# Attention block on one core: queries and keys projected without padding by pairs of head groups, turned by a transposing DMA; values by group pairs

## The chip, the cores and the metric

The kernel runs on one core of one Trainium2 chip. The metric is the device time of one execution in microseconds (us); less is better. The engines are TensorE (PE; its weight loads are listed as PEld), VectorE (DVE), ScalarE (ACT), GpSimd (POOL) and SyncE (SP), which issues the DMAs of this kernel.

## The reference

A transformer block over 2048 rows of 640 elements: layer norm, attention with 32 heads of 20 elements, and a gated bilinear layer of width 1728, both with a residual. All inputs are bf16.

```python
x = A_x                                             # 1 x 2048 x 640
h = x + _A_ref(_layernorm(x), A_wqkv, A_wo)
h2 = h + _B_ref(_layernorm(h), B_w_gate, B_w_up, B_w_down)

def _A_ref(x, wqkv, wo):                            # H = 32, Dh = 20
    q, k, v = ...                                   # (x @ wqkv), split and by heads
    scores = einsum("bhqd,bhkd->bhqk", q, k) * Dh ** -0.5
    o = einsum("bhqk,bhkd->bhqd", softmax(scores), v)
    return o.reshape(B, S, D) @ wo

def _B_ref(x, w_gate, w_up, w_down):
    return ((x @ w_gate) * (x @ w_up)) @ w_down
```

## The kernel before, in words

**Layout.** The 32 heads form eight groups of four (`NG`, `HPG`). A head has a slot of 32 partitions (`SLOT`), 20 of them used, so a group fills 128 partitions. `kT[g]` holds the keys of group g turned: 128 partitions by 2048 rows. `qa[g]` holds the queries of rows 0 to 1535 in the same way, `qb[g]` those of rows 1536 to 2047. `vx[t]` holds the values of the 128 rows t, heads side by side, each with a column of ones behind its 20 elements, which gives the sums of the softmax. `lnT` holds the normed rows turned: five chunks of 128 columns of the model by 2048 rows.

**Projections.** For queries and keys the weights are first padded from 20 to 32 columns a head (`wpad`, filled by `pad_half` on ACT and POOL), so that one projection comes out in slots. `job_proj(m, g, ch)` makes the queries (m = 0) or keys (m = 1) of group g for block ch of 512 rows: five matmuls with `wpad` as weights and 512 columns of `lnT`, and one DVE eviction at L310 from PSUM to `kT` or `qa`/`qb`. The eviction adds a constant: keys get one in partition 20 of each slot (`one_row`), queries 544 (`shift_row`), so that each score comes out raised by 544. `job_V(t, half)` makes the values of 128 rows for sixteen heads: five matmuls with `lnT` as weights and 320 columns, cast into `vx[t]` at L268 by `evac`. All these jobs, and the transposes on PE, use the single PSUM bank of pool `mip`; the first keys of group 1 use `accp`.

**Rows.** The layer norm of a block of 512 rows runs in pieces on DVE, with a few small steps on POOL (`gen_ln`, L206 to L259). The normed rows of the blocks 0 and 1 are turned on PE (`job_T`, L281), those of the blocks 2 and 3 by transposing DMAs from SP (`turn`, L910).

**Scores.** A tile holds 1536 columns of scores, three units of 512 columns or six of 256. `emit_S` issues its score matmuls (L550) into one of two PSUM tiles `sc`; ACT takes the exponential of a whole tile (L566) into an `E` buffer; `emit_AV` multiplies with `vx` into `acc` (L787). For some tiles DVE takes the last 512 columns in place of ACT, by four operations of its own (`emit_x`: L602, L612, L613, L607). Whether it does is decided by `x_takes`: among other things DVE must not be behind PE by the program's own clock, at most two such pieces may be open, and for groups that are divided over blocks none is started while row statistics are left (`aux`) or in the last `X_CHUNK` tiles of the group.

**Order.** The order of all instructions is fixed when the program is built. The row block of queries 0 comes first ("pass 0"): for its groups 0 to 3 the keys are taken in four blocks of 512 rows, all four groups in block 0, then in block 1, and so on, with partial results in `parts` (memory of `qa`); then groups 4 to 7 over all keys; then the other passes. The loop over tiles places jobs from the queue `jobs` between the score matmuls as long as its clock (`at`) says that PE would be idle; `ensure` runs jobs at once where a tile needs their result. For each kind of work the clock has a cost, such as 216 ns a matmul of 512 columns. Sums of the softmax go through DRAM to rows and back (`norm`: L658, L659, L671, L674 on SP, L669 and L677 on DVE). The loads of `wo` (L983) are issued in the last part of pass 0, and `spill` copies the queries to DRAM for a fallback.

## Time and profile before

| | |
|---|---|
| Time, median of 3 runs | 898.12 us (897.2 to 899.1) |
| Profiled execution | 895.98 us, span 894.2 us |
| PE busy | 800.1 us (89%) |
| DVE busy | 760.1 us (85%) |
| ACT busy | 853.5 us (95%) |
| POOL busy | 33.6 us (4%) |
| Moved by DMA | 60.48 MB |

The span runs from the first to the last instruction of the profiled execution; the time has some 1.8 us around it. A share is that of the span in which an engine ran at least one instruction. Lines such as L310 are those of the kernel before.

### The profile page before, as it was taken

The page shows a single profiled execution, that of the slowest core. Times are in us where ns is not written, and L with a number is a line of the kernel's source. Part 1 is how long each engine was busy: PE and PEld are TensorE (multiplying, and loading weights), DVE is VectorE, ACT ScalarE, POOL GpSimd, SP SyncE. Part 2 cuts the span into 40 slices and gives each one's busy share as a digit, 9 for nine tenths or more (in the row PEclk, how much of TensorE's full clock was granted, in tenths as well). Part 3 has the DMA queues.
Part 4 walks back from the last instruction along what each step waited for, and adds up shares of the span by engine and source line. Part 5 has one row for each costly group of instructions (what it writes and reads, how often), then busy time and mean ns, then how long its engine had stood idle before and what let it go on. Part 6 is the DMA issues. An engine that isn't in the chain of part 4 may idle for free.

```text
span 894.2 us, 21880 instructions
## 1 busy us (share of the span) xinstructions
PE 800.1 (89%) x8861; PEld 373.1 (42%) x8919; DVE 760.1 (85%) x1415; ACT 853.5 (95%) x719; POOL 33.6 (4%) x126
## 2 busy tenths in 40 slices
PE   7888999988988899989899988988889999889997
PEld 5333233222223344544344544433434455435466
DVE  7778899999999999799999998999899888994443
ACT  6999999999999999999999999999999999999951
POOL 4100000000001100001000000001000000100000
PEclk9999999999999999999999999999999999999999
DMA  6030010011024655432224334111542203011310
GB/s 199 23 65 3 1 29 25 15 37 28 14 67 120 132 147 190 121 89 67 58 60 109 81 96 109 45 31 30 132 111 74 73 14 79 12 34 39 89 38 18
DMA packets 112107, 60.48 MB, mean 68 GB/s; under 512 B 39320, under 2 KB 108996, under 8 KB 112000
## 3 DMA queue, kind: packets, MB, share of 16 engines
q1 hardware_dynamic: 112000, 59.01, 25.3%
q8 instruction: 72, 1.18, 0.5%
q14 instruction: 35, 0.29, 0.1%
HBM read 48.09 MB, written 7.28 MB: 62 GB/s over the span
## 4 chain that ended last, share of the span: by engine, by line
ACT 61%; PE 15%; issue 15%; DVE 9%; DMA 1%; ACTq 0%; DVEq 0%
ACT E L566 49%; ACT El L566 11%; PE sc L550 3%; PE mi L1162 2%; PE acc L787 2%; PE f L1144 2%; PE mi L303 1%; DVE xv L602 1%; DVE xt L612 1%; PE f L1211 1%; DVE xt L613 1%; PE mi L1044 1%; DVE xe L607 1%; PE mi L318 1%; DVE u L1167 1%
## 5 line engine op out<-in xcount | busy, mean ns | idle before, releaser
L566 ACT ACTIVATE E<-sc 128x1536 bf16<-128x1536 f32 (+1 forms) x560 | 696.1, 1397 | 2.5 <-PE sc L550 1.7
L550 PE MATMUL sc<-qa,kT 32*128 32x256 bf16 (+1 forms) x2176 | 203.0, 318 | 27.9 <-ACT E L566 14.8
L550 PEld LDWEIGHTS <-kT 32*128 32x128 bf16 x3136 | 86.1, 91 | 225.9 <-issue 194.3
L602 DVE TENSOR_SCALAR xv<-sc 128x512 f32<-128x512 f32 x194 | 133.9, 690 | 46.1 <-PE sc L550 43.0
L566 ACT ACTIVATE El<-sc 128x1536 bf16<-128x1536 f32 (+1 forms) x123 | 159.8, 1378 | 0.3 <-PE sc L550 0.3
L787 PE MATMUL acc<-E,vx 128*32 128x256 bf16 (+1 forms) x2255 | 156.9, 314 | 1.2 <-DVE vx L268 0.6
L607 DVE SCALAR_TENSOR_TENSOR xe<-xt,xv 128x512 int16<-128x512 f32 x194 | 131.2, 682 | 0.9
L613 DVE SCALAR_TENSOR_TENSOR xt<-xt,xv 128x512 f32<-128x512 f32 x194 | 130.2, 681 | 0.8
L612 DVE SCALAR_TENSOR_TENSOR xt<-xv 128x512 f32<-128x512 uint16 x194 | 129.1, 680 | 0.4 <-DVE ri L669 0.2
L303 PE MATMUL mi<-lnT,wp 128*128 128x512 bf16 x280 | 82.7, 381 | 8.1 <-DVE qa L310 3.4
L787 PEld LDWEIGHTS <-vx 128*32 128x32 bf16 x3136 | 61.9, 96 | 61.1 <-issue 59.5
L550 PE MATMUL sc<-qb,kT 32*128 32x256 bf16 (+1 forms) x960 | 68.4, 280 | 6.9 <-ACT E L566 4.2
L1211 PE MATMUL mi<-wd,hh 128*128 128x320 bf16 x378 | 65.5, 301 | 1.2 <-DVE xr L1215 1.1
L1162 PE MATMUL mi<-ln2T,wg 128*128 128x256 bf16 x390 | 56.7, 274 | 8.6 <-DVE u L1167 7.6
L1162 PE MATMUL mi<-ln2T,wu 128*128 128x256 bf16 x390 | 55.7, 274 | 7.2 <-DVE hh L1170 7.0
L787 PE MATMUL acc<-El,vx 128*32 128x256 bf16 (+1 forms) x579 | 59.5, 292 | 0.3 <-ACT El L566 0.3
L787 PE MATMUL acc<-xe,vx 128*32 128x256 bf16 (+1 forms) x302 | 55.4, 306 | 0.3 <-issue 0.3
L1211 PEld LDWEIGHTS <-hh 128*128 128x128 bf16 x448 | 37.9, 97 | 29.4 <-issue 18.1
L1162 PEld LDWEIGHTS <-wg 128*128 128x128 bf16 x390 | 33.7, 97 | 30.0 <-issue 25.9
L303 PEld LDWEIGHTS <-wp 128*128 128x128 bf16 x310 | 24.8, 97 | 50.6 <-issue 38.5
L1162 PEld LDWEIGHTS <-wu 128*128 128x128 bf16 x390 | 33.7, 97 | 28.3 <-issue 25.2
L1170 DVE TENSOR_TENSOR hh<-mi,u 128x512 bf16<-128x512 f32 x49 | 33.7, 688 | 13.3 <-PE mi L1162 12.7
(141 smaller groups left out, 618.4 us busy)
## 6 DMA issues: line engine op xcount, KB each, us to landing
wu<-in_B_w_up_dram SPq DMA_DIRECT2D x38, 320.0 KB
wg<-in_B_w_gate_dram SPq DMA_DIRECT2D x37, 320.0 KB
bc<-scr SPq DMA_DIRECT2D x60, 64.0 KB
bc<-scr SPq DMA_DIRECT2D x108, 32.0 KB
qsp<-qa SPq DMA_DIRECT2D x8, 384.0 KB
xr<-in_A_x_dram SPq DMA_DIRECT2D x16, 160.0 KB
out_dram<-xr SPq DMA_DIRECT2D x14, 160.0 KB
wd<-in_B_w_down_dram SPq DMA_DIRECT2D x13, 160.0 KB
```

The source lines that it names most:

```text
L303: nc.tensor.matmul(ps[:], lhsT=wslice(m, g, c), rhs=lnT[:, c, ch * QB:(ch + 1) * QB], start=(c == 0), stop=(c == KT - 1))
L550: nc.tensor.matmul(sc[:, o:o + w], lhsT=kT[g][SLOT * j:SLOT * (j + 1), kt * P:(kt + 1) * P], rhs=q_of(g, b, c0, w)[SLOT * j:SLOT * (j + 1) ...
L566: exps = nc.scalar.activation(e[:, 0:n_act], sc[:, 0:n_act], ACT.Exp, bias=EXP_BIAS, scale=SM_SCALE)
L602: took = nc.vector.tensor_scalar(v[:], ps, X_SCALE, X_BASE, ALU.mult, ALU.max)
L607: nc.vector.scalar_tensor_tensor(e[:], t[:], X_R, v[:], ALU.mult, ALU.add)
L612: lambda: nc.vector.scalar_tensor_tensor(t[:], u, X_P, u, ALU.add, ALU.mult),
L613: lambda: nc.vector.scalar_tensor_tensor(t[:], t[:], X_Q, u, ALU.add, ALU.mult),
L787: nc.tensor.matmul(acc["t"][SLOT * j:SLOT * (j + 1), 0:w], lhsT=vx[kt][:, VS * h:VS * h + SLOT], rhs=e, start=(acc["n"][j] == 0), stop=(ac ...
L1144: nc.tensor.matmul(ps[:, 0:n], lhsT=st["w", fp][k][:, c, f_cols(fp, f2)], rhs=st["ln2T"][:, c, c0:c0 + n], start=(c == 0), stop=(c == KT - 1))
L1162: nc.tensor.matmul(ps[:, f2 * n:(f2 + 1) * n], lhsT=st["w", fp][k][:, c, f_cols(fp, f2)], rhs=st["ln2T"][:, c, c0:c0 + n], start=(c == 0), ...
L1170: nc.vector.tensor_tensor(st["hh"][fp][:, :, c0 % HW:c0 % HW + n], two(ps[:, 0:2 * n]), two(u[:, 0:2 * n]), ALU.mult)
L1211: nc.tensor.matmul(ps[:, 0:HALF], lhsT=st["hh"][f // 2][:, f % 2, t * P % HW:t * P % HW + P], rhs=late["Wd"][f][:, cs], start=(f == 0), st ...
```

## The change

Queries and keys of the first block of 512 rows and of the groups 0 and 1 are projected as before (`DIRECT = 2`), with padded weights for these two groups alone. All others are made by `job_pair` for two groups and 256 rows at once: `lnT` is the weights, the unpadded query or key weights of eight heads (160 columns) are streamed, ten matmuls in all. DVE casts the 320 columns into one of five padded tiles `stages`, in which the constant already stands in element 20 of each slot, and SP turns the tile by a transposing DMA of 128 x 512 into `kT`, `qa` or `qb`. These now hold two groups each, in an order of row tile, group, row. The constant is 23.25 on both sides, so that the scores are raised by 23.25 squared. Values are made by `job_vp` for two groups and 256 rows, ten matmuls of 160 columns, with one cast. The queries of the later row blocks are made for the groups 4 to 7 first. The program's clock takes a turned tile as readable 2.4 us after its eviction (`MOVE_NS`). The unpadded weights get memory of their own in place of that of `E` and `wo`; POOL sets the constants of the five tiles and some more of the values' borders.

```diff
+DIRECT = 2
+STAGES = 5
+PAIR = 2 * HPG * DH
...
+MOVE_NS = 2400
...
-SHIFT = 544.0
+ROOT_SHIFT = 23.25
...
-    qa = [qkp.tile([P, QA], BF16, name=f"qa{g}", tag=f"qa{g}") for g in range(NG)]
-    qb = [qkp.tile([P, QB], BF16, name=f"qb{g}") for g in range(NG)]
-    kT = [qkp.tile([P, S], BF16, name=f"kT{g}") for g in range(NG)]
-    vx = [vp.tile([P, VW], BF16, name=f"vx{t}") for t in range(NT)]
+    qa = [qkp.tile([P, NT - TPB, 2, P], BF16, name=f"qa{k}") for k in range(NG // 2)]
+    qb = [qkp.tile([P, TPB, 2, P], BF16, name=f"qb{k}") for k in range(NG // 2)]
+    kT = [qkp.tile([P, NT, 2, P], BF16, name=f"kT{k}") for k in range(NG // 2)]
+    vx_all = vp.tile([P, NT, VW], BF16, name="vx")
+    vx = [vx_all[:, t, :] for t in range(NT)]
...
-    wqk = [ep.tile([P, EW], BF16, name="E") for c in range(KT)]
-    wpad = [ra.tile([P, 2, H, SLOT], BF16, name=f"wp{c}") for c in range(KT)]
+    wqk = [[ra.tile([P, 2, HALF], BF16, name=f"wqk{hf}{c}") for c in range(KT)] for hf in range(2)]
+    wpad = [ra.tile([P, 2, DIRECT * HPG, SLOT], BF16, name=f"wp{c}") for c in range(KT)]
+    stages = [ra.tile([P, 4 * HPG, SLOT], BF16, name=f"st{k}") for k in range(STAGES)]
...
-        nc.gpsimd.memset(vx[t][:, hh_ * VS:hh_ * VS + SLOT - VS], 1.0)
+        for h0 in range(2 * HPG, H, 2 * HPG):
+            nc.gpsimd.memset(vx[t][:, h0 * VS:h0 * VS + SLOT - VS], 1.0)
...
+    for st in stages:
+        nc.gpsimd.memset(st[:, :, DH:VS], ROOT_SHIFT)
+        nc.gpsimd.memset(st[:, :, VS:SLOT], 0.0)
...
-    def job_proj(m, g, ch):
+    def job_proj(m, g):
...
-                nc.vector.tensor_scalar(kT[g][:, ch * QB:(ch + 1) * QB] if m else q_of(g, ch, 0, QB), ps[:],
-                                        (one_row if m else shift_row)[:, 0:1], None, ALU.add)
+                nc.vector.tensor_scalar(kT[g // 2][:, 0:TPB, g % 2, :] if m else q_of(g, 0, 0, QB), by_tile(ps[:]), shift_row[:, 0:1], None, ALU.add)
...
+    def job_pair(key, m, gp, tt, dst):
...
+        st = stages[staged["n"] % STAGES]
+        staged["n"] += 1
+        lo = gp % 2 * PAIR
+        for k in range(2):
+            for c in range(KT):
+                nc.tensor.matmul(ps[:, k * PAIR:(k + 1) * PAIR], lhsT=lnT[:, c, (2 * tt + k) * P:(2 * tt + k + 1) * P],
+                                 rhs=wqk[gp // 2][c][:, m, lo:lo + PAIR], start=(c == 0), stop=(c == KT - 1))
+                if k and c == KT - 1:
+                    evac("dve", st[:, :, 0:DH], ps[:, 0:2 * PAIR].rearrange("p (h e) -> p h e", e=DH), 408, 68)
+                    nc.sync.dma_start(dst.rearrange("p t g k -> p (t g) k"), st[:].rearrange("p h e -> p (h e)"), transpose=True)
+                    read_at[key] = at["dend"] + MOVE_NS
+                yield 68
...
+    def job_vp(gp, tt):
...
+                nc.tensor.matmul(ps[:, k * PAIR:(k + 1) * PAIR], lhsT=lnT[:, c, (2 * tt + k) * P:(2 * tt + k + 1) * P],
+                                 rhs=wv[c][:, h0 * DH:h0 * DH + PAIR], start=(c == 0), stop=(c == KT - 1))
...
-    for c in range(KT):
-        pad_half(c, 1)
...
+            add(("k0", 1), job_proj(1, 1))
+            values(0)
+            for k in range(2):
+                add_q(0, 1, k)
+            add_k(1, 0)
+            one_T()
+            add_k(1, 1)
+            one_T()
+            values(1)
             one_T()
             one_T()
+        else:
+            values(0)
+            for k in range(2):
+                add_k(1, 2 * ch + k)
+            values(1)
...
+    for gp in range(G1 // 2, NG // 2):
+        for k in range(2):
+            add_q(0, gp, k)
+        for tt in range(NT // 2):
+            add_k(gp, tt)
+            add(("vp", gp, tt), job_vp(gp, tt))
...
-    for b in range(1, NB):
-        for g in range(NG):
-            add(("q", b, g), job_proj(0, g, b))
+    for hf in (1, 0):
+        for b in range(1, NB):
+            for k in range(4):
+                add_q(b, 2 * hf + k // 2, k % 2)
```

154 lines of the change are left out of this document (73 added, 81 removed).

## Prediction

> **What bounds the kernel now.** I read the page's busy times, then the span cut into stages, then who waited for whom, and last the groups of instructions and the timelines of single engines.
>
> ```profile
> PE 800.1 (89%) x8861; PEld 373.1 (42%) x8919; DVE 760.1 (85%) x1415; ACT 853.5 (95%) x719; POOL 33.6 (4%) x126
> ACT 61%; PE 15%; issue 15%; DVE 9%; DMA 1%; ACTq 0%; DVEq 0%
> 15.00:60.00 45.00, 38.64 (x293) 14.23 (x297) 34.85 (x85) 43.17 (x33) 8.47 (x22) 1.00 0.18 45
> 60.00:131.00 71.00, 63.98 (x490) 22.74 (x493) 59.05 (x103) 71.00 (x59) 0.00 (x0) 1.00 0.08 19
> 131.00:256.00 125.00, 113.39 (x824) 34.94 (x838) 117.61 (x197) 124.57 (x104) 0.00 (x0) 1.00 0.09 21
> ```
>
> The first line is engines over the whole span, the second the shares of the chain that ended last. Each stage row is: stretch, its length, then busy us of PE, PEld, DVE, ACT, POOL, the granted clock, DMA share, GB/s. ACT, which only takes exponentials there, is busy for 71.00 of 71 us and 124.57 of 125. The three stages are those in which queries, keys and values are projected; only in the first does ACT idle, 1.83 us of 45. So a projection that gets cheaper on PE moves nothing by itself. What moves the end is how many score columns DVE takes off ACT by its own exponential (L602, L612, L613, L607), and any wait that ACT gets or loses.
>
> ```profile
> L566 ACT ACTIVATE E<-sc 128x1536 bf16<-128x1536 f32 x402 | 569.1, 1516 | 2.5 <-PE sc L550 1.7 <-PE acc L787 0.4
> L566 ACT ACTIVATE E<-sc 128x1024 bf16<-128x1024 f32 x158 | 167.7, 1092 | 0.0
> 15.00:60.00 45.00, 0.00 (x0) 1.00 0.18 45
> 60.00:131.00 71.00, 9.77 (x15) 1.00 0.08 19
> 131.00:256.00 125.00, 21.28 (x31) 1.00 0.09 21
> ```
>
> The first two rows are ACT's groups with shapes kept apart (busy us, mean ns): a tile whose last 512 columns DVE took costs ACT 1516 - 1092 = 424 ns less. The other three are the same stages for L602 alone: DVE starts none of its exponentials before 60 us, 15 in the next 71 us, 31 in the last 125. In the last stage DVE is busy for 117.61 of 125 us, so there it is DVE time that limits them. Between 15 and 131 us the rule of `x_takes` limits them (none while row statistics are in `aux`, and for the divided groups not in the last three tiles of a group): DVE idles there for 22 of 116 us.
>
> **Part by part: DVE.** 64 projections of four heads by 512 columns are made now; four of them stay as they are (groups 0 and 1, first block), 60 become 60 pair jobs of eight heads by 256 rows.
>
> ```profile
> L310 DVE TENSOR_SCALAR kT<-mi,one_row 128x512 bf16<-128x512 f32 x30 | 22.4, 746 | 5.1 <-PE mi L303 4.6
> L310 DVE TENSOR_SCALAR qa<-mi,shift_row 128x512 bf16<-128x512 f32 x23 | 17.1, 744 | 2.5 <-PE mi L303 2.3
> L268 DVE CAST vx<-mi 128x320 bf16<-128x320 f32 x32 | 15.6, 488 | 3.5 <-PE mi L318 3.3
> 71.51 0.68 DVE L612 SCALAR_TENSOR_TENSOR xt<-xv 128x512 f32<-128x512 uint16 x1
> 72.11 0.48 DVE L268 CAST vx<-mi 128x320 bf16<-128x320 f32 x1
> 72.51 0.68 DVE L607 SCALAR_TENSOR_TENSOR xe<-xt,xv 128x512 int16<-128x512 f32 x1
> 73.11 0.68 DVE L613 SCALAR_TENSOR_TENSOR xt<-xt,xv 128x512 f32<-128x512 f32 x1
> ...
> 74.12 0.69 DVE L602 TENSOR_SCALAR xv<-sc 128x512 f32<-128x512 f32 x1 [0.33 <-PE sc L550]
> 74.73 0.74 DVE L310 TENSOR_SCALAR kT<-mi,one_row 128x512 bf16<-128x512 f32 x1
> 75.39 0.68 DVE L607 SCALAR_TENSOR_TENSOR xe<-xt,xv 128x512 int16<-128x512 f32 x1
> ```
>
> Records overlap their neighbours by some 0.08 us, so I take the distance from start to start where DVE had no wait: 0.66 us for the 512-column eviction (74.73 to 75.39), 0.40 us for a cast of 320 columns (72.11 to 72.51), 0.60 us for a step of the exponential. The new eviction is a cast of 320 columns into a padded tile, for which L268 is the nearest row. DVE gains 60 x (0.66 - 0.40) = 15.6 us. One exponential is four steps, 4 x 0.605 = 2.42 us; 15.6 / 2.42 = 6.4. The values stay 32 evictions of 320 columns. Jobs that end sooner in the first 131 us pull later ones into DVE's idle time there, so most of the gain turns up behind 131 us, where DVE is the limit. I take 6 of the 6.4, since DVE is busy for 94% of that stage: 6 x 0.424 = 2.5 us off ACT. The bounds are 0 (the planner finds no tile for them) and 10 (also 10 us of the idle 22 us become usable, because the statistics end sooner): 4.2 us.
>
> **PE.**
>
> ```profile
> 7.58 0.45 PE L281 MATMUL mi<-ident,xs 128*128 128x128 bf16 x5 [1.29 <-DVE xs L259]
> 16.80 1.25 PE L303 MATMUL acc<-lnT,wp 128*128 128x512 bf16 x5
> 18.31 0.85 PE L318 MATMUL mi<-wv,lnT 128*128 128x320 bf16 x5
> L318 PEld LDWEIGHTS <-lnT 128*128 128x128 bf16 x160 | 14.1, 97 | 19.6 <-issue 16.2
> L281 PE MATMUL mi<-ident,xs x30: 217/219/230, 7.6 to 41.4; 128*128 128x128 bf16 x30
> ```
>
> A run of five takes four spacings and one duration. For 128 columns that is (0.45 - 0.219) / 4 = 58 ns with a new weight load for each. The five of 512 columns take 1.25 us, a spacing near 217 ns, the five of 320 near 137 ns. Between 58 and 137 ns, 160 columns come to 71 ns by a straight line. Ten of them are 0.71 us against 1.08 us: 60 x 0.37 = 22 us less PE time. The 32 value jobs go from five matmuls to ten, 0.68 to 0.71 us, 1 us more. On the end this is worth nothing directly, since ACT is never short of scores after 60 us; it is what lets the jobs end sooner.
>
> [...]
>
> **The transposes.** Each pair job now ends in a transposing DMA of 128x512 on SP, 60 in all. The rows' own transposes are the nearest thing, 128x640 each.
>
> ```profile
> L910 SPq DMA_TRANSPOSE lnT<-xs x8: 1199/1217/1322, 43.0 to 65.2; - x8
> 66.40:66.60 0.20, 1.00 0.94 179
> ...
> 67.00:67.20 0.20, 1.00 0.94 176
> 192.66 6.92 SPq L983 DMA_DIRECT2D wo<-in_A_wo_dram x16
> 131.00:256.00 125.00, 28.32 (x38) 1.00 0.09 21
> ```
>
> The first row is the issue time on SP (minimum, median, maximum ns, first and last start); the next two are the first and the last of four slices in which the DMA engines were busy with the last of them (share, GB/s): issued at 65.2, moved from 66.4 to 67.2. So 1.22 us of issue and 0.8 us of transfer; four fifths of both is 0.97 + 0.64 = 1.6 us from eviction to landing. The program assumes 2.4 us; I keep 1.6 to 2.4. SP gets 60 x 0.97 = 58 us of issue over 241 us. What stands ahead in SP's queue delays a transpose: the longest such block is the 16 loads of `wo`, 6.92 us. Behind it DVE could stand, because the five padded tiles are reused in turn. The last row is L310 in the last stage: 38 evictions in 125 us, one in 3.3 us; at twice that pace five tiles still last 8 us. I cost it at 0, bounded by 2 us if the pace is three times as high. The sums' trips through DRAM share that queue too, but are planned 6 us ahead; 0, within the same bound.
>
> **The start.**
>
> ```profile
> 3.75 0.33 POOL L194 MEMSET vx<- 128x11 bf16 x1
> 3.80 0.29 POOL L195 MEMSET vx<- 128x12 bf16 x1
> 7.19 2.42 POOL L200 COPY wp<-E 128x640 bf16<-128x640 bf16 x3 [3.10 <-DMA E<-in_A_wqkv_dram]
> 30.38 0.38 PE L550 MATMUL sc<-qa,kT 32*128 32x512 bf16 x1 [0.62 <-DVE kT L310]
> 30.86 14.88 ACT L566 ACTIVATE E<-sc 128x1536 bf16<-128x1536 f32 x11 [1.05 <-PE sc L550]
> 43.58 0.74 DVE L310 TENSOR_SCALAR kT<-mi,one_row 128x512 bf16<-128x512 f32 x1
> 45.15 0.39 PE L550 MATMUL sc<-qa,kT 32*128 32x512 bf16 x3
> ```
>
> POOL gets 42 more memsets in front of the weight pads. At 0.05 us each that is 2.1 us, and it stood idle for 3.10 us there; the pads halve. Cost 0; without that cover, 2.1 us. ACT loses 1.05 us at 30.86, because the scores of group 2 waited for keys that had just been made. The work ahead of those keys shrinks from 7.0 to about 6 us on PE, the evictions from 0.66 to 0.40, the landing adds 1.6 to 2.4. I take half of the idle away, 0.5 us (bounds: all of it, or 1 us more).
>
> **The sum.** 2.5 + 0.5 = 3.0 us. The profiled execution took 895.98 us (span 894.2 us and 1.78 around it), so 893.0; the median of the runs shown, 898.12, lies 2.1 above it, so 895.1. About 0.2%, 1.8 us, is what a measurement here tells from no change.
>
> **Rivals.** *Keys come late (slower).* In the first four blocks of 512 rows a pair's keys are needed soon after they are made: once in block 0 (groups 2 and 3), twice in each of blocks 1 to 3, seven places. At 30.38 the lead was nil, at 45.15, where the next block's keys are first read, 45.15 - 44.32 = 0.8 us. Where the lead stays under 1.6 us, PE stands at the scores, and ACT behind it; one such wait of 0.62 us cost ACT 1.05. At 1.0 us a place, 7 us, less the 2.5 us of DVE: +4.5, 902.6. It decides from the point at which pair jobs end less than 1.6 us ahead of their scores. Against it: per block, four value jobs and four key projections, 7.0 us of PE time, become eight jobs of 0.7 us, and each needs less of the one PSUM bank, so the lead should grow by over 1 us. [...]
>
> *DVE's time cannot be used (no change).* The tiles that DVE may take are limited by its two open tiles and by PE being ahead, not by its time; then 0 to 3 exponentials more, -0 to -1.3 us, 897.5. For it: DVE waits at L602 for scores. Against it: 94% busy.
>
> *PE gets no lighter (no change).* If each weight load of 97 ns sets the pace, 920 narrow matmuls cost 26 ns more each than 71, 24 us, all that was saved; jobs end no sooner, half the exponentials come, -1.3 us, 896.8. The burst at 58 ns speaks against it.
>
> *More than the sum.* Ten exponentials and no early idle, -4.2 - 1.0: 892.9.
>
> **The numbers.** The forecast 895.1 has 0.48, the larger gain 0.09; the two that end within 0.2% have 0.12 and 0.04; late keys 0.20, of which a fifth (0.04) would cancel the gain only; and queueing on SP 0.07, where the 2 us fall due at two or three places, 895.1 + 5 = 900.1. So faster 0.57, same 0.20, slower 0.23. The range takes in the larger gain with its bounds and most of the late keys: 892.0 to 902.6. The forecast's own range is 893.5 to 896.5.
>
> **What would show it.** Right: some 200 exponentials at L602 instead of 194, most of the new ones between 131 and 256 us; the 60 evictions near 490 ns each; 60 more transposes issued in about 1 us each; ACT idle under 1.8 us between 15 and 60 us; PE busy about 20 us less. Wrong: ACT waiting for `sc` behind a DMA into `kT` or `qa` in the first 100 us; DVE waiting for a DMA that reads the padded tiles; PE's runs of ten well over 0.9 us; the count at L602 unchanged.

## The result, and the profile after

The changed kernel takes 924.46 us in the median (922.8 to 927.28), against 898.47 us for the kernel before beside it: a ratio of 1.029 with an interval of 1.027 to 1.032. The prediction had 895.1 us. The change costs 26 us where I forecast a gain of 3. Executions of one program differ along with their mean granted clock: the kernel before took 895.45 us at 1.0 and 904.51 at 0.988, and the four of the changed kernel had 0.968 to 0.972.

The profiled execution took 922.8 us, with a span of 921.0. From here on lines are those of the kernel after: scores L594 (before L550), exponentials L611 (L566), products with the values L832 (L787), DVE's own exponential L647, L657, L658, L652 (L602, L612, L613, L607), pair jobs L344, values L365, DVE's casts L274, transposing DMAs L348. From its page, the busy times, the row of granted clocks and ACT's main group:

```profile
PE 825.6 (90%) x9474; PEld 410.0 (45%) x9474; DVE 749.9 (81%) x1427; ACT 855.4 (93%) x719; POOL 32.4 (4%) x163
PEclk9989999979999999998999999899999999999899
L611 ACT ACTIVATE E<-sc 128x1536 bf16<-128x1536 f32 (+1 forms) x559 | 694.5, 1380 | 24.9 <-PE sc L594 24.4
```

ACT does the same work (855.4 us, before 853.5), but now it stands 24.4 us in front of scores that are not there; before, that group's wait was 1.7 us. The clock row has 7 and 8 where before every digit was 9. And PE, whose work was to shrink by 20 us, is listed as busy 25.5 us longer. A part of that is only the record: the page before has 58 fewer matmuls than weight loads (8861 and 8919), the page after has all of them, and a run below with the work of before and all its records (only the order changed) lists 812.0 us. The three stages, with the columns of before:

```profile
15.00:60.00 45.00, 36.29 (x373) 18.04 (x372) 34.29 (x89) 43.18 (x32) 5.86 (x18) 0.94 0.40 76
60.00:131.00 71.00, 64.98 (x715) 35.12 (x714) 59.97 (x109) 70.39 (x59) 0.00 (x0) 0.99 0.24 46
131.00:256.00 125.00, 107.48 (x1013) 48.28 (x1011) 104.47 (x191) 113.61 (x94) 0.00 (x0) 0.95 0.30 58
```

The last two of them for L647, the first step of DVE's exponential, alone:

```profile
60.00:131.00 71.00, 10.97 (x16) 0.99 0.24 46
131.00:256.00 125.00, 21.11 (x31) 0.95 0.30 58
```

The start is as before: ACT idles 45 - 43.18 = 1.82 us, then 0.61 us. Between 131 and 256 us it idles 11.39 us, where before it idled 0.43, and the granted clock averages 0.95. DVE is freed as intended (104.47 us busy, before 117.61), yet it starts 31 of its exponentials there, as many as before.

The table load behind ACT's last exponential starts at 879.0 us; before it started at 854.24. Of these 24.8 us, 23.2 are longer waits for scores (25.2 us with those in front of `El`, before 2.0). What follows takes 42.0 us instead of 40.0. So the question is why scores come late.

One place shows how a stand comes about. The timeline of SP's queue from 173 us (start, us, instruction):

```profile
173.28 2.50 SPq L348 DMA_TRANSPOSE qa<-st  x2
175.88 1.61 SPq L716 DMA_DIRECT2D scr<-ri  x1
178.81 1.70 SPq L719 DMA_DIRECT2D bc<-scr  x4
180.61 1.41 SPq L1024 DMA_DIRECT2D wo<-in_A_wo_dram  x4
182.12 1.20 SPq L348 DMA_TRANSPOSE qa<-st  x1
183.42 1.56 SPq L1024 DMA_DIRECT2D wo<-in_A_wo_dram  x4
185.11 1.19 SPq L348 DMA_TRANSPOSE qa<-st  x1
```

DVE's timeline (with the wait in front in brackets):

```profile
184.63 0.49 DVE L274 CAST st<-mi 128x320 bf16<-128x320 f32 x1 [3.06 <-DMA qa<-st]
187.63 0.49 DVE L274 CAST st<-mi 128x320 bf16<-128x320 f32 x1 [1.19 <-DMA qa<-st]
```

PE's timeline:

```profile
182.06 0.39 PE L594 MATMUL sc<-qa,kT 32*128 32x512 bf16 x3
185.17 1.49 PE L344 MATMUL mi<-wqk,lnT 128*128 128x160 bf16 x10 [2.72 <-DVE st L274]
186.59 0.61 PE L594 MATMUL sc<-qa,kT 32*128 32x512 bf16 x3
```

ACT's timeline:

```profile
187.25 1.02 ACT L611 ACTIVATE E<-sc 128x1024 bf16<-128x1024 f32 x1 [3.04 <-PE sc L594]
189.91 1.02 ACT L611 ACTIVATE E<-sc 128x1024 bf16<-128x1024 f32 x1 [1.64 <-PE sc L594]
```

And slices of 1 us, whose third figure from the end is the granted clock:

```profile
183.00:184.00 1.00, 0.00 (x0) 0.00 (x0) 0.00 (x0) 1.00 (x1) 0.00 (x0) 1.00 0.65 129
184.00:185.00 1.00, 0.00 (x0) 0.00 (x0) 0.37 (x1) 0.21 (x1) 0.00 (x0) 0.51 0.23 46
...
193.00:194.00 1.00, 1.00 (x9) 0.72 (x7) 1.00 (x2) 0.55 (x1) 0.00 (x0) 0.50 0.50 97
...
195.00:196.00 1.00, 0.82 (x13) 0.69 (x12) 0.98 (x3) 0.97 (x1) 0.00 (x0) 1.00 0.54 104
```

DVE wants to cast into a padded tile whose transpose has not been read out yet: the tile was filled at 172.04 us, but that transpose stood in SP's queue behind a trip of the sums (175.88 to 180.51 us) and loads of `wo` until 182.12, and DVE's wait ends 2.4 us after its issue. DVE stands 3.06 us; the next pair job of PE needs the one bank that this cast frees and stands 2.72 us; the scores behind it in PE's order are late, and ACT stands 3.04 us. While PE stands, its clock falls to 0.50 and stays there for ten slices. At half clock three score matmuls take 0.61 us instead of 0.39 and the pair job 1.49 instead of some 0.86, so ACT waits again: 1.64 us behind a second, shorter stand (DVE's 1.19 us for the next tile's transpose), then 0.50 and 0.57 us with no wait for a DMA in between.

Slices at half clock lie in eight stretches before the end of the exponentials, from 54, 140, 184, 379, 413, 464, 594 and 867 us; in the profiled execution before there were none. Each lasts 3.4, 6.8 or 10.2 us in the trace's clock records. Of ACT's 25.2 us of waits, 15.0 us are waits that touch such a stretch (4.7 of them the two behind the stands just shown), 1.7 lie just ahead of one, 8.5 elsewhere. The trace shows one of two things ahead of each stretch: a stand such as the one above (140 behind DVE's wait of 1.93 us for a broadcast of the sums, with PE standing 1.90 and then 1.00 us, 184, and 379 behind PE's wait of 1.87 us for a load of `wg`), or a shortage of full-array work (54, and the ends of the passes at 413, 464, 594, 867, where PE has mostly scores, products with the values and the tiny matmuls of the sums). In the 4 us ahead of these five, matmuls of 128 rows and 128 columns are busy for 0.1 to 1.6 us; from 50 to 850 us the mean is 1.9 us in 4. What amount it takes is not shown: from 289 to 293 us they are busy for 0.6 us, and the clock stays at 1.00, as it does behind a stand of 1.61 us at 313 us.

Both kernels take their 683 exponentials in the same order, so the start of the n-th (counted from 0) can be compared. The changed kernel is level with the one before until the 80th (120 us). From the 80th to the 100th it loses 4.3 us (the stretch at 140), from the 120th to the 150th 8.0 (184), from the 280th to the 320th 5.2 (379), over the last 42 exponentials 4.4, and over all the rest 3.0. So the loss is made at a few places, not by every tile.

### The profile page after: what moved, and what is told of

Its sections match the earlier page's. It is cut to its first block, busy times and chain, and to the rows that moved or that the text cites. A ratio compares the mean times of both kernels' runs of the same rounds, so it can differ in the third digit from the quotient of the medians.

```text
span 921.0 us, 23257 instructions
## 1 busy us (share of the span) xinstructions
PE 825.6 (90%) x9474; PEld 410.0 (45%) x9474; DVE 749.9 (81%) x1427; ACT 855.4 (93%) x719; POOL 32.4 (4%) x163
## 4 chain that ended last, share of the span: by engine, by line
ACT 54%; PE 21%; issue 13%; DVE 6%; DMA 4%; SPq 1%; ACTq 0%; DVEq 0%
ACT E L611 43%; ACT El L611 11%; PE sc L594 5%; PE acc L832 3%; PE mi L344 3%; PE f L1186 2%; PE mi L544 2%; PE mi L1204 1%; DVE st L274 1%; PE f L1253 1%; PE mi L1086 1%; DMA wg<-in_B_w_gate_dram 1%; DMA xs<-in_A_x_dram 1%; DVE xt L658 1%; PE mi L365 1%
## 5 line engine op out<-in xcount | busy, mean ns | idle before, releaser
L611 ACT ACTIVATE E<-sc 128x1536 bf16<-128x1536 f32 (+1 forms) x559 | 694.5, 1380 | 24.9 <-PE sc L594 24.4
L594 PE MATMUL sc<-qa,kT 32*128 32x256 bf16 (+1 forms) x2176 | 207.6, 325 | 21.2 <-ACT E L611 15.9
L594 PEld LDWEIGHTS <-kT 32*128 32x128 bf16 x3136 | 85.4, 92 | 212.1 <-issue 166.2
L647 DVE TENSOR_SCALAR xv<-sc 128x512 f32<-128x512 f32 x197 | 135.6, 688 | 46.3 <-PE sc L594 43.1
L611 ACT ACTIVATE El<-sc 128x1536 bf16<-128x1536 f32 (+1 forms) x124 | 163.9, 1404 | 0.8 <-PE sc L594 0.8
L832 PE MATMUL acc<-E,vx 128*32 128x256 bf16 (+1 forms) x2243 | 160.0, 320 | 0.2 <-ACT E L611 0.2
L652 DVE SCALAR_TENSOR_TENSOR xe<-xt,xv 128x512 int16<-128x512 f32 x197 | 132.7, 681 | 0.8
L658 DVE SCALAR_TENSOR_TENSOR xt<-xt,xv 128x512 f32<-128x512 f32 x197 | 131.6, 680 | 0.5
L657 DVE SCALAR_TENSOR_TENSOR xt<-xv 128x512 f32<-128x512 uint16 x197 | 131.1, 682 | 0.4
L832 PEld LDWEIGHTS <-vx 128*32 128x32 bf16 x3136 | 62.5, 96 | 59.6 <-issue 56.8
L594 PE MATMUL sc<-qb,kT 32*128 32x256 bf16 (+1 forms) x960 | 69.2, 283 | 5.5 <-ACT E L611 3.7
L344 PE MATMUL mi<-wqk,lnT 128*128 128x160 bf16 x600 | 58.2, 239 | 13.1 <-DVE st L274 8.0
L1204 PE MATMUL mi<-ln2T,wg 128*128 128x256 bf16 x410 | 60.6, 277 | 10.1 <-DVE u L1209 6.4
L544 PE MATMUL mi<-kT,ident 128*128 128x512 bf16 x212 | 65.0, 388 | 4.1 <-DVE hh L1212 1.4
L1204 PE MATMUL mi<-ln2T,wu 128*128 128x256 bf16 x410 | 58.2, 273 | 10.1 <-DVE hh L1212 8.8
L1253 PE MATMUL mi<-wd,hh 128*128 128x320 bf16 x364 | 62.6, 302 | 1.5 <-DVE xr L1257 1.5
L832 PE MATMUL acc<-xe,vx 128*32 128x256 bf16 (+1 forms) x304 | 60.9, 314 | 0.0
L344 PEld LDWEIGHTS <-lnT 128*128 128x128 bf16 x600 | 43.8, 100 | 36.9 <-issue 36.5
L832 PE MATMUL acc<-El,vx 128*32 128x256 bf16 (+1 forms) x589 | 60.0, 295 | 0.0
```

What stands on the lines that cost most here:

```text
L344: nc.tensor.matmul(ps[:, k * PAIR:(k + 1) * PAIR], lhsT=lnT[:, c, (2 * tt + k) * P:(2 * tt + k + 1) * P], rhs=wqk[gp // 2][c][:, m, lo:lo ...
L544: nc.tensor.matmul(ps[:], lhsT=ident[:], rhs=kT[0][:, 0:2].rearrange("p t g k -> p (t g k)"), start=True, stop=True)
L594: nc.tensor.matmul(by_tile(sc[:, o:o + w]), lhsT=kT[g // 2][SLOT * j:SLOT * (j + 1), kt, g % 2, :], rhs=q_of(g, b, c0, w)[SLOT * j:SLOT * ...
L611: exps = nc.scalar.activation(e[:, 0:n_act], sc[:, 0:n_act], ACT.Exp, bias=EXP_BIAS, scale=SM_SCALE)
L647: took = nc.vector.tensor_scalar(v[:], ps, X_SCALE, X_BASE, ALU.mult, ALU.max)
L652: nc.vector.scalar_tensor_tensor(e[:], t[:], X_R, v[:], ALU.mult, ALU.add)
```

## The experiments

Three theories compete. **C (clock):** the change takes work from PE, PE runs out of projections early, and its clock halves. **Q (queue):** 60 transposes in SP's queue hold the five padded tiles; DVE and then PE stand. **P (plan):** the program orders all instructions by its own clock, any changed cost moves all that follows, and a part of the loss belongs to the order and not to the operations. In the tables "waits" are ACT's waits for scores in us, between 15 and 256 us and from there to 880; "tail" is the time from the last exponential to the end.

**The `wo` loads off SP.** Edit of the changed kernel:

```diff
-                nc.sync.dma_start(wo[g][SLOT * j:SLOT * j + DH, :], A_wo[DH * h:DH * h + DH, :])
+                nc.gpsimd.dma_start(wo[g][SLOT * j:SLOT * j + DH, :], A_wo[DH * h:DH * h + DH, :])
```

> The changed kernel with the 32 loads of wo issued from GpSimd in place of SyncE, which takes some 12 us of issue out of the queue of the transposes. Theory Q (the one SyncE queue holds up the padded tiles and the sums, DVE waits, PE waits behind DVE): DVE's waits for a transpose near 181 to 188 us (3.1 + 1.2 us) go, and with them the half-clock stretch of 184 to 194 us; 5 to 8 us less than 924.5, so 917 to 919. Theory C (the lighter projections leave PE too little work, and its granted clock halves wherever it runs short): the other seven half-clock stretches stay, so still over 914. If the queue were all of it, 900.

Measured: 918.24 us, ratio 1.023 (1.019 to 1.027), about 6 us better than the changed kernel, with the same order of instructions on PE. DVE no longer waits for a DMA that reads a padded tile at all, and the stretch at 184 us is gone. Between 131 and 200 us ACT's waits fall from 10.3 to 3.6 us. But the stretches at 54 and 140 us stay. So Q is worth about 6 us here, and it isn't most of the loss.

**A stricter rule for idle matmuls.** The program already issues idle matmuls: two at a time at L544 where it finds no job for PE, and one at L590 ahead of a tile's scores where by its own clock PE has had less than `FULL_NS` of full-array work, or less than `ALL_NS` of any, in the last 2.08 us. By their weight loads there were 126 + 18 of them before (the trace lacks 33 matmul records of the 126) and 212 + 27 after. The edit makes the rule of L590 stricter:

```diff
-WARM, LEAD, COOL_FROM = 58, 3, 30
+WARM, LEAD, COOL_FROM = 58, 3, 12
-FULL_IN, FULL_NS, ALL_NS = 2083, 300, 760
+FULL_IN, FULL_NS, ALL_NS = 2083, 500, 1000
```

> The changed kernel with the program's rule for warming matmuls made stricter: they start at tile 12 in place of 30, and are placed when full-array work in the last 2.08 us is under 500 ns (was 300) or, with part-array work, under 1000 ns (was 760). Theory C: the half-clock stretches at 54, 412, 463, 593 and 866 us go, those behind DVE's or a DMA's wait (139, 184, 378) stay; ACT's wait for scores falls from 24 to about 14 us; time 908 to 914. Theory Q: the stretches are a consequence of DVE's waits, so nothing changes by more than 3 us, or it gets slower by the added matmuls.

> Both edits of the two runs above together. Theories C and Q both at work, independent: the gains add, 902 to 908. C alone: as the stricter warming by itself. Q alone: as the moved loads by themselves.

Measured: alone 927.68 us, ratio 1.033 (1.028 to 1.038); together with the moved `wo` loads 916.35, 1.020 (1.016 to 1.024). Alone it is no help. It gave PE no more work either: 56 idle matmuls at L590 instead of 27, but 176 at L544 instead of 212, 232 in all instead of 239. So these two runs say little about C. With `wo` moved, the granted clock of the profiled execution rises to 0.989 (0.978 with `wo` moved alone), but the gain over moving `wo` alone is within the scatter. Waits on DMAs remain: PE 4.1 us for `ln2T`, DVE 4.4 for the sums.

**Less work on PE, and no DMA.** Edit of the kernel before, three of five matmuls in each projection except those of groups 0 and 1 in the first block, so each of the others lacks two fifths of its contraction:

```diff
-        for c in range(KT):
+        n_c = KT if g < 2 and ch == 0 else 3
+        for c in range(n_c):
```

> The kernel before with three of the five matmuls in each projection of queries and keys, the four of groups 0 and 1 in the first block excepted: 648 ns of PE in place of 1080 for 60 jobs, 26 us less PE work, with no new DMA and the old evictions. It leaves out two fifths of the contraction. Theory C: PE runs short here too, the clock halves in several stretches, and the kernel gets slower than before by 5 to 20 us. Theory Q: no transposes, no queue, so the time is that of before within 3 us, or a little less.

Measured: 906.69 us, ratio 1.009 (1.006 to 1.012): with 120 projection matmuls fewer (the program put in 83 idle ones more), and no transposing DMA added, it is 8 us slower. Its clock around 54 us, in slices of 1 us:

```profile
53.00:54.00 1.00, 0.60 (x11) 0.19 (x9) 0.90 (x3) 1.00 (x2) 0.29 (x2) 1.00 0.85 161
54.00:55.00 1.00, 0.39 (x3) 0.10 (x3) 0.34 (x1) 1.00 (x2) 0.76 (x5) 0.66 0.55 104
55.00:56.00 1.00, 0.61 (x3) 0.20 (x3) 0.07 (x1) 1.00 (x2) 0.90 (x1) 0.50 0.33 63
...
60.00:61.00 1.00, 1.00 (x8) 0.22 (x11) 0.00 (x0) 1.00 (x1) 0.00 (x0) 0.50 0.50 96
```

PE's timeline ahead of it:

```profile
49.50 0.82 PE L304 MATMUL mi<-lnT,wp 128*128 128x512 bf16 x2
50.25 0.39 PE L551 MATMUL sc<-qa,kT 32*128 32x512 bf16 x3
51.32 0.39 PE L551 MATMUL sc<-qa,kT 32*128 32x512 bf16 x3 [0.67 <-ACT E L567]
52.66 0.39 PE L551 MATMUL sc<-qa,kT 32*128 32x512 bf16 x3 [0.95 <-ACT E L567]
```

From 50.3 us PE has nothing but scores and products of 32 rows or columns of the array, waits for ACT, and 4 us later its clock halves, in the same slice and with the same 0.66 and 0.50 as in the changed kernel. No instruction on PE had waited for a late DMA there. ACT waits 4.5 us at `E` and 2.0 at `El`, more than a half of it in waits that touch the half-clock stretches. None of the seven profiled executions with full projections (the kernel before, and the runs below with the order, the values, the transposes, the short evictions and the two nudges) has a stretch near 54 us. So less work on PE is enough to halve the clock there, with no transpose about. Its price is another matter: at the 60th exponential, behind this stretch, this kernel is 0.6 us ahead of the kernel before, as the changed one is 0.2 ahead there. It loses its 8 us later, more than a half of it in the last 42 exponentials and the tail.

No gap of PE in the 4 us ahead was longer than 0.95 us, here and in the changed kernel alike (there PE was busy for 2.25 of those 4 us), so the clock halves without a long stand too.

**The order alone, and the values alone.** Edits of the kernel before:

```diff
-    for b in range(1, NB):
-        for g in range(NG):
-            add(("q", b, g), job_proj(0, g, b))
+    for hf in (1, 0):
+        for b in range(1, NB):
+            for g in range(G1 * hf, G1 * (hf + 1)):
+                add(("q", b, g), job_proj(0, g, b))
```

```diff
-            add(("v", t, 1), job_V(t, 1))
+            add(("vp", g // 2, tt), job_vp(g // 2, tt))
...
```

> The kernel before with one thing of the change alone: the queries of the later row blocks are made for the groups 4 to 7 first. Same work on every engine, same DMAs, only another order from about 190 us on. Theory C (too little PE work lets the granted clock fall): no change, 897 to 900, no half-clock stretch before the last microseconds. Theory P (the order of before happens to keep the clock up, any other order falls below the gate somewhere): two to four half-clock stretches behind 190 us and 4 to 10 us more, as with the lighter projections.

> The kernel before with the values made by group pairs (ten matmuls of 160 columns for 256 rows) and in the order that this gives; queries and keys as before. PE time and evictions are the same. Theory C and theory Q: the same time within 3 us. Theory P: 4 to 10 us more, with half-clock stretches. A PE that runs ten narrow matmuls slower than five wide ones would show as runs of over 0.9 us.

Measured: the order 899.13 us, 1.001 (0.999 to 1.003), nothing, although its profiled execution has two half-clock stretches (397 and 649 us) with PE's work as before, so such stretches come without lighter projections too; the values by group pairs 904.53, 1.007 (1.004 to 1.009). The second has no transposes, waits of only 4.0 us in all and one half-clock stretch at 573 us. Its DVE makes 190 exponentials instead of 194 (4 x 0.424 = 1.7 us), its tail is 42.3 us instead of 40.0, and DVE waits 4.6 us for sums. What of this is the value jobs' own cost and what their order's, this run cannot tell.

**Three padded tiles.**

```diff
-STAGES = 5
+STAGES = 3
```

> The changed kernel with three padded tiles in place of five. Theory Q (DVE stands at its eviction until SyncE has turned an earlier tile, PE behind DVE): DVE's waits for a transpose at its eviction grow from 5.8 us to 15 to 30 us, ACT's wait between 20 and 220 us from 14 to over 20 us, and the time is 6 to 15 us over 924.5. Theory C alone: within 3 us of it.

Measured: 931.04 us, 1.037 (1.033 to 1.041). DVE's largest wait for a DMA, in the list of waits (us in total, times, longest), here and then in the changed kernel:

```profile
DVE st L274 <- DMA qa<-st: 12.5, 8, 2.8
```

```profile
DVE st L274 <- DMA qa<-st: 5.8, 3, 3.1
```

With two tiles fewer this wait grows by 6.7 us and the time by 6.6. The program's order changes in part with it, so the near equality proves little, but the wait itself is Q's, and five tiles were already too few in that queue. More than five were not tried.

**The sums' trips off SP as well.** Edit: beside `wo`, the four steps through DRAM of each `norm` are issued by GpSimd.

```diff
-        nc.sync.dma_start(sums[:], asb[DH:P:SLOT, 0:w])
+        nc.gpsimd.dma_start(sums[:], asb[DH:P:SLOT, 0:w])
...
```

> The changed kernel with the loads of wo and also the sums' four trips through DRAM issued from GpSimd; SyncE is left with transposes, rows and weights. Theory Q: DVE's wait at 135 us for the sums, and the half-clock stretch of 139 to 146 us behind it, go as well; ACT's wait from 131 to 200 us falls from 3.6 us (with wo alone moved) to under 1; 4 to 7 us less than the 918.2 of that run, 911 to 914. Theory C: the stretches at 54 us and behind 350 us stay, so not under 908. If the GpSimd queue takes much longer for the trips, DVE waits there and the time rises instead.

Measured: 927.54 us, 1.030 (1.024 to 1.036), worse than `wo` alone by 0.7%. DVE now waits 11.0 us for the sums and 9.4 for their broadcasts. The trips got slower by GpSimd, so this says nothing about SP's queue.

**Work given back to PE.** Edits on top of the moved `wo` loads: two idle matmuls of 512 columns ahead of every pair job; then with the stricter rule (500 and 1000); then the idle ones only for keys, and later row blocks' queries, of groups 4 to 7, whose results are not needed soon.

```diff
+        for _ in range(2):
+            nc.tensor.matmul(ps[:], lhsT=ident[:], rhs=kT[0][:, 0:2].rearrange("p t g k -> p (t g k)"), start=True, stop=True)
+            yield 216
```

```diff
-        for _ in range(2):
+        for _ in range(2 if gp > 1 and (m or key[1]) else 0):
```

> The changed kernel with wo loaded from GpSimd and two idle matmuls of 512 columns put in front of each pair job, so that a pair job costs PE about 1.1 us, as a projection did before. Theory C: PE has its work back, the half-clock stretch at 54 us goes and so do those behind DVE's short waits; ACT's wait for scores up to 256 us falls from 7.4 us (wo moved alone) to 2 to 4; 904 to 912 in place of 918.2. Theory Q: only the queue matters and PE's load does not, so 916 to 920, or more, since jobs end later.

> The kernel with filled pair jobs and wo from GpSimd, and the stricter rule for warming matmuls (500 and 1000 ns in place of 300 and 760; the first tile for it stays 30). Theory C: the half-clock stretches at the ends of the later passes (about 412, 463, 593, 866 us) go as well, those behind a DMA's wait stay; 900 to 907. Theory P (the late stretches come from an order that no longer fits and not from too little work): no better than without the rule.

> The changed kernel with wo from GpSimd, the stricter rule for warming matmuls (500 and 1000 ns), and the two idle matmuls only in front of pair jobs whose result is not needed soon: keys of the groups 4 to 7, and their queries of the later row blocks. The early keys and the queries of pass 1 keep their lead. If too little PE work between 60 and 256 us and SyncE's queue are the causes there, and filling failed before only because it made early keys late: ACT's wait for scores is 3 to 5 us up to 256 us, 3 to 5 us behind it, 902 to 907 in all. If filling costs by itself, it stays over 914.

| kernel | us | ratio | waits 15 to 256 | waits 256 to 880 | tail |
|---|---|---|---|---|---|
| before | 898.47 | | 1.7 | 0.3 | 40.0 |
| after | 924.46 | 1.029 (1.027 to 1.032) | 13.8 | 11.3 | 42.0 |
| `wo` moved | 918.24 | 1.023 (1.019 to 1.027) | 7.4 | 10.3 | 42.4 |
| + filled everywhere | 927.73 | 1.034 (1.031 to 1.037) | 22.1 | 6.5 | 42.3 |
| + stricter rule | 923.19 | 1.028 (1.025 to 1.031) | 20.9 | 5.1 | 42.8 |
| filled late only, stricter rule | 905.79 | 1.007 (1.005 to 1.009) | 6.9 | 2.2 | 44.0 |

In this order, filling every pair job makes the time worse, for a reason of its own. The largest of PE's waits for a DMA in the kernel that is filled everywhere:

```profile
PE sc L597 <- DMA kT<-st: 8.9, 3, 3.8
```

and one of them in its timeline:

```profile
38.83 0.38 PE L597 MATMUL sc<-qa,kT 32*128 32x512 bf16 x1
41.96 0.61 PE L597 MATMUL sc<-qa,kT 32*128 32x512 bf16 x2 [2.74 <-DMA kT<-st]
```

The early keys come late, and ACT loses 13.6 us before 60 us. In the same kernel ACT's waits between 131 and 200 us, the stage of the stand above, fall to 0.7 us (10.3 after, 3.6 with `wo` moved), and the granted clock of that stage is 1.00 (0.90 and 0.95). With the fill left out where keys are needed at once, both come together, and the list of ACT's waits has

```profile
ACT E L614 <- PE sc L597: 9.1, 13, 1.8
```

instead of 24.4 us. This kernel still has all 60 transposes and pair jobs, and takes back three quarters of the loss (ratio 1.007 instead of 1.029). As each step also gives another plan, how much of this is the clock and how much the order is taken up below.

**The transposes alone, and DVE's relief alone.** Edits of the kernel before: a transpose of every new 128x512 of keys or queries on SP into scratch that nobody reads; and evictions of 320 of the 512 columns, the other 192 filled by a GpSimd copy of finished ones, so that 192 columns of keys and queries are stand-ins.

```diff
+                    nc.sync.dma_start(turned_to[staged["n"] % len(turned_to)][:], new, transpose=True)
```

```diff
+                nc.vector.tensor_scalar(new[:, 0:cut], ps[:, 0:cut], (one_row if m else shift_row)[:, 0:1], None, ALU.add)
+                if cut < QB:
+                    nc.gpsimd.tensor_copy(new[:, cut:QB], new[:, 0:QB - cut])
```

> The kernel before with one thing added: behind each of the 60 projections that the change replaces, SyncE turns the 128x512 result into a scratch tile that nobody reads (two such tiles in turn). PE, DVE and ACT do what they did. Theory Q: the transposes alone hold up the sums and wo in SyncE's queue; DVE waits 3 to 8 us for the sums, 3 to 8 us over 898. Theory C: the queue matters only through the padded tiles that DVE refills, which this kernel doesn't have; within 2 us of 898.

> The kernel before with DVE's relief alone: its 60 evictions take 320 of their 512 columns, and the program's clock counts 408 in place of 640 ns; GpSimd copies the other 192 columns from the first ones (so these rows of queries and keys are repeats and not their own). PE and SyncE do what they did. If 15 us of DVE time turn into exponentials, as the prediction's sum had it: 199 to 200 at L602 in place of 194, and 2 to 3 us less, 895 to 896. If x_takes places no more tiles whatever DVE has left: 194 to 197 of them, and 897 to 900.

Measured: the transposes 900.21 us, 1.003 (1.000 to 1.005); they cost some 2 us when nothing waits for them, at the edge of what can be told. The execution in the trace took 906.9, the highest of its runs, with four half-clock stretches and 10.2 us of waits, so this kernel is itself near that edge. The relief of DVE 907.85 us, 1.010 (1.008 to 1.012), slower, and the reason is instructive. Up to 256 us it does what the prediction said: 18 exponentials of DVE between 60 and 131 us and 34 behind, where before there were 15 and 31, and from the 60th to the 210th exponential ACT is some 2 to 3 us ahead of the kernel before. Then the lead melts: at the 640th exponential it is 0.9 us behind, at the last 5.5, and the tail is 2.6 us longer. Behind 256 us DVE makes 145 exponentials instead of 149, and ACT waits 5.1 us for scores instead of 0.3, 0.8 us of it in a half-clock stretch at 847 us. Behind 256 us the two kernels have the same work. That fits P; this run alone does not show it.

**The plan alone.** The kernel before, with a cost in the program's clock changed and no work: the eviction of a projection planned 8 ns shorter; or, in another kernel, the change between kinds of matmuls planned 4 ns longer. The second edit was then made in the changed kernel, in the one with the `wo` loads moved, and in the one filled late.

```diff
-                dve(640, 216)
+                dve(632, 216)
```

```diff
-S_NS, S_EXP, SWITCH = 226, 497, 96
+S_NS, S_EXP, SWITCH = 226, 497, 100
```

> The kernel before with one cost of the program's clock changed: a projection's eviction is planned at 632 ns in place of 640; the work is the same, only the order moves. By the built order 98 matmuls of the last product (L1211, tile f) are left for the end in place of 70, two more halves of 14. Theory P (any other plan loses several us, above all in the last 42 exponentials and the tail): 902 to 908 us, the tail 43 to 44 us in place of 40.0, one to three half-clock stretches. C and Q alone: 898, since neither PE's work nor SP's queue changed.

> The kernel before with another cost changed: SWITCH (the change between kinds of matmuls) 100 ns in place of 96. Same work; here the built order leaves the same 70 matmuls in the tail. P as located at the end: 898 to 901, tail near 40; P as a loss of any new plan wherever: 902 to 908; C and Q alone: 898.

> The best version so far (wo loads on GpSimd, stricter rule, idle matmuls only ahead of pair jobs whose results aren't needed soon) with SWITCH 100, which leaves 70 matmuls in the tail in place of 84. If what was left of that version's loss, 7 us, is the plan's end (P), some 3 to 5 us come back: 901 to 903, tail near 41 in place of 44.0. If it is the clock and the queue: 905 to 907.

> The changed kernel with the wo loads on GpSimd and SWITCH 100: 70 matmuls in the tail in place of 84, 176 idle matmuls in place of 212. P: 2 to 5 us less than with the wo loads alone, 913 to 916, since C's stretches at 54 and 140 us stay. If the plan's end doesn't matter: 918.

> The changed kernel with SWITCH 100 in place of 96 and nothing else: the wo loads stay on SP. Its instructions on PE and DVE are in the same order as in the kernel with the wo loads moved and SWITCH 100 (901.66 us). If the plan is nearly all of the loss: 902 to 905. If the queue's 6 us (Q) are a cost of their own in any plan: 906 to 909, with DVE standing some 5 us for padded tiles between 180 and 190 us and a half-clock stretch there. If the change's own parts cost more than the plan: over 915.

| kernel | us | with `SWITCH` 100 | ratio with it |
|---|---|---|---|
| before | 898.47 | 902.15 | 1.004 (1.001 to 1.006) |
| before, eviction planned at 632 | 902.76 | | (1.005, 1.003 to 1.007) |
| after | 924.46 | 907.24 | 1.009 (1.006 to 1.011) |
| after, `wo` moved | 918.24 | 901.66 | 1.003 (1.001 to 1.005) |
| after, filled late, stricter rule | 905.79 | 899.71 | 1.001 (0.999 to 1.003) |

One number of the plan, moved by 4 ns, takes 17 us off the changed kernel, and 16.6 off it with `wo` moved; no work is dropped but idle matmuls (at L544 212 become 176, at L590 27 become 24), and four more tiles go to DVE, which is 4 x 0.424 = 1.7 of the 17 us. The same number costs the kernel before 4 us, and the other nudge costs it 4 as well. So with `SWITCH` 100 on both sides the change costs 5 us (907.24 against 902.15), and nothing with `wo` moved (901.66). The late fill with the stricter rule, which took off 12 us at first (918.24 to 905.79), takes off 2 there (901.66 to 899.71), so most of those 12 us were the order's and not the clock's. I had sized P at a few us; it is the largest part of the result.

How the order does it is seen exponential by exponential, counted from 0, each time less that of the kernel before (us from the start of the span, in the profiled executions):

| start of exponential no. | 60 | 100 | 150 | 210 | 320 | 640 | 682 | tail |
|---|---|---|---|---|---|---|---|---|
| time before | 95.4 | 144.4 | 205.8 | 278.2 | 411.4 | 798.6 | 853.1 | 40.0 |
| after | -0.2 | +4.1 | +12.8 | +11.7 | +18.6 | +20.5 | +24.9 | +2.1 |
| after, `wo` moved | +1.3 | +5.9 | +5.7 | +4.8 | +9.5 | +10.8 | +16.5 | +2.4 |
| after, `SWITCH` 100 | +0.8 | +2.0 | +9.0 | +6.9 | +7.4 | +7.9 | +7.4 | +0.2 |
| after, `wo` moved, `SWITCH` 100 | +1.5 | +2.7 | +3.1 | +1.0 | +1.5 | +2.1 | +1.6 | +1.2 |
| before, eviction planned at 632 | -0.5 | +0.2 | 0.0 | -0.7 | -0.6 | +0.6 | +2.8 | +2.0 |
| before, `SWITCH` 100 | -0.1 | 0.0 | -0.6 | +0.9 | +2.3 | +4.7 | +4.2 | +2.2 |
| before, short evictions | -2.2 | -2.1 | -2.2 | -2.2 | -1.0 | +0.9 | +5.5 | +2.6 |

With the other order the stands at 140 and 379 us and the loss in the last 42 exponentials do not occur. DVE's largest wait for a DMA in the kernel with `SWITCH` 100 and the `wo` loads on SP:

```profile
DVE on L722 <- DMA bc<-scr: 6.9, 4, 4.8
```

and ACT's wait for scores in it:

```profile
ACT E L611 <- PE sc L594: 10.9, 14, 4.8
```

The same two with `wo` moved as well:

```profile
DVE on L722 <- DMA bc<-scr: 1.9, 2, 1.1
```

```profile
ACT E L611 <- PE sc L594: 5.1, 11, 0.8
```

In that last kernel, the group of L647, then the third stage over all engines, and the same for L647 alone:

```profile
L647 DVE TENSOR_SCALAR xv<-sc 128x512 f32<-128x512 f32 x201 | 138.6, 689 | 41.8 <-PE sc L594 37.3
```

```profile
131.00:256.00 125.00, 112.68 (x1096) 50.32 (x1094) 113.96 (x209) 124.37 (x104) 16.20 (x32) 1.00 0.34 68
```

```profile
131.00:256.00 125.00, 23.50 (x35) 1.00 0.34 68
```

These two have the same order of instructions on PE and on DVE, so they separate Q from P cleanly. With the loads of `wo` on SP one stand of 4.8 us is left, DVE behind a broadcast of the sums that came late, and not behind a padded tile as I had expected; a half-clock stretch of 6.8 us begins at 205 us, and from the 120th to the 150th exponential ACT loses 7.1 us against 0.5. In the medians it is 5.6 us (4.8 by the ratios to the kernel before). Both kernels have 201 exponentials of DVE. Without the queue's stand, ACT is busy 124.37 of 125 us behind 131 us and DVE takes 35 tiles there, and in the table above that kernel is never more than 3.1 us behind the kernel before.

P is not a matter of the end alone, as one reading of it said: with `SWITCH` 100 the kernel before loses from the 150th exponential on. And the tail is not explained by the count of matmuls left for it, as I had expected: with 98 left (eviction planned at 632) it is 41.9 us, with 70 left (`SWITCH` 100 in the kernel before) 42.2.

No version of the changed kernel beat the kernel before; filled late with `SWITCH` 100 cannot be told from it.

## Why the prediction was wrong

**The sum has no term for the order.** This is the step that failed most. It priced each operation against the order of the kernel before and took that order as given, apart from "jobs that end sooner ... pull later ones into DVE's idle time". In fact every cost that the change touches gives the program another order of all that follows, and the order that came out met the stands at 140 and 379 us and a bad end. 17 of the 26 us go away with another order of the same work, idle matmuls aside. No rival of the prediction had this case, and its range could not hold it.

**"On the end this is worth nothing directly, since ACT is never short of scores after 60 us."** PE's spare time was treated as free. The row of granted clocks of the page before, 9 throughout, was a condition that I read as a constant: with the projections lighter, PE runs out of full-array work (0.1 us of it in the 4 us ahead of the stretch at 54 us), and the three stands of PE of 1.9 to 2.7 us are followed by 3.4 to 10.2 us at half clock. The stands at 140, 184 and 379 us and the stretches behind them cost 4 to 8 us each; 15.0 us of ACT's waits touch such stretches, 4.7 of them due to the stands at 184 themselves, and no run parts the one from the other. The expected 20 us less of PE time came as more, 825.6 us against the 812.0 of the order-only run, with matmuls at half clock and 95 more idle ones.

**"At twice that pace five tiles still last 8 us. I cost it at 0, bounded by 2 us."** The sum's 0 and its bound of 2 us failed here. The queueing rival had the place (the loads of `wo`) and, at 5 us, nearly the size, but a chance of only 0.07. It is worth 6 us in the one order and 5.6 in the other, mostly at a single place. The pace was not even: at the stand DVE's casts came 1.6 us apart (176.55, 178.16 and 179.76 us), while SP issued no transpose from 175.8 to 182.1. The half clock behind the stand was not in the price.

**Transposes at "four fifths" of 1.22 us.** They are listed at

```profile
L348 SPq DMA_TRANSPOSE kT<-st x30: 1188/1191/2111, 25.5 to 162.4; - x30
L348 SPq DMA_TRANSPOSE qa<-st x22: 1188/1210/2009, 22.1 to 215.1; - x22
L348 SPq DMA_TRANSPOSE qb<-st x8: 1216/1216/1510, 191.0 to 220.4; - x8
```

so a transpose of 512 columns is issued in 1.2 us, as long as one of 640: 72 us of SP instead of 58, which made the queue longer.

**DVE: "I take 6 of the 6.4".** In the changed kernel there are 197 exponentials, not 200, and 31 behind 131 us as before, so the rival of unusable time seems to hold. It does not: with `wo` moved and `SWITCH` 100 there are 201 (192 in the kernel before with `SWITCH` 100), 35 of them there, and ACT is busy 850.3 us, 3.2 us less than before. The term of 2.5 us was of the right size, and even in the short evictions alone it was visible for 200 us. In the changed kernel the stands and the half clock of PE fall into that stage; that they took it is likely and not shown apart.

What held: the sizes of the single operations and the start. From PE's timeline a run of a pair job, and from the groups of instructions DVE's casts, both in the changed kernel:

```profile
71.72 0.87 PE L344 MATMUL mi<-wqk,lnT 128*128 128x160 bf16 x10
```

```profile
L274 DVE CAST st<-mi 128x320 bf16<-128x320 f32 x60 | 29.3, 488 | 15.8 <-PE mi L344 9.5 <-DMA qa<-st 5.8
```

A run of ten at full clock takes 0.85 to 0.87 us; less a last duration near 0.24, nine spacings of 68 to 70 ns, where I had 71. The cast takes 488 ns. The early keys were not late (PE waited 0.4 us for `kT`), so that rival did not decide; but it was real, as the filled kernel showed at 13.6 us.

**What stays open.** Why this one order meets the stands at 140 and 379 us and the poor end, and whether that of the kernel before is unusually good, no run shows: only a few nearby plans were measured. Nor do the runs part the order as such from the 39 idle matmuls fewer and the four tiles more for DVE that came with it. A half-clock stretch that begins between 30 and 57 us stays in the changed kernel (54 us) and in its three versions with `SWITCH` 100 (54 us, 55 with `wo` moved, 30 and 57 filled late), and the order-only run (397 and 649 us) and the nudged ones (570; 651 and 869 us) have stretches of their own later on, with PE's work as before. What remains of the change when `wo` is moved and the plan fits, 3 us (1.001 to 1.005) slower than before, is within what two empty nudges did to the kernel before (4 us each), so the sign of the operations' own net effect is not settled.

## What to carry to other kernels

In a kernel whose order is computed from cost estimates, changing an operation changes the order too: before a loss or a gain of a few per cent is put down to the operation, move one estimate by a little in both kernels and see how far the time goes; here that was 4 us in one and 17 us in the other. Read the granted clock in the stage as a condition that the present work keeps up, and price a stand with the half-clock stretch behind it (here 1.9 to 2.7 us of PE, then 3.4 to 10.2 us). Where a ring of buffers is put behind a queue that issues in order, add up what the queue issues in its worst burst, the other engines' waits in it included (here 6.3 us between two transposes).

## What the hardware showed that I had not expected

- The granted clock of the changed kernel falls in one step from 1.00 to 0.50 and, ahead of the end, stays there for 3.4, 6.8 or 10.2 us, also at 54 us, where PE's longest idle gap in the 4 us ahead was 0.95 us: scores of 32 rows and products of 32 columns, with PE busy for 2.25 of those 4 us, did not hold it up.
- A transposing DMA of 128x512 takes as long to issue on SP (medians of 1.19 to 1.22 us) as one of 128x640 (1.22 us in the kernel before).
- The small trips of the sums through DRAM take DVE 20.4 us of waits in total when issued by GpSimd, against 4.5 us when issued by SP (4.2 of them for the broadcasts).
